# Scores and values' products in one burst, and four seams re-ordered, in a chunked attention with a gated FFN

## The chip, the cores and the metric

The kernel runs on one core of a Trainium2 chip. The core has a matmul engine (PE, with a weight loader PEld), a vector engine (DVE), an activation engine (ACT), a general engine (POOL) and a queue engine that issues DMAs (SP). The metric is the device time of one launch in microseconds. The kernel before takes 894.38 us, the median of three runs (893.72, 894.38 and 894.40).

## The reference

Inputs are q, k and v [8, 8, 576, 64], w_gate and w_val [512, 1536] and w_out [1536, 512], all float32. Attention is within chunks of 64 tokens; its output, with the heads side by side, is the input of a gated feed-forward layer.

```python
scores = scale * np.matmul(q_c, k_c.transpose(0, 1, 2, 4, 3))   # chunks of 64 tokens, scale 1/8
scores = scores - np.max(scores, axis=-1, keepdims=True)
attn = np.exp(scores)
attn = attn / (np.sum(attn, axis=-1, keepdims=True) + 1e-09)
out = np.matmul(attn, v_c)
...
x = np.ascontiguousarray(attn_out.transpose(0, 2, 1, 3)).reshape(B * S, H * D)   # [4608, 512]
g = x @ w_gate
silu = g * (1.0 / (1.0 + np.exp(-g)))
val = x @ w_val
return (silu * val @ w_out).astype(np.float32)
```

## The kernel before

**Tiles.** The 4608 tokens are nine blocks b = 0 to 8 of N = 512, each of T = 4 output tiles of 128 tokens. The hidden width 1536 is NF = 12 slices f of 128. A float32 operand is split into a high and a low part (`hh`, `hl` for h), and every product is three matmuls: low by high, high by low, high by high. `project` (L535) adds one slice of a block to its four output tiles: for each tile t three matmuls of 512 columns (L541, L542, L543). The output tiles are four banks of PSUM (`ps_o`); two more banks are `ps_a`, two `ps_gv`.

**Stages.** Blocks 0 and 1 are worked first; from slice SEVEN = 4 on, two blocks share seven products (`seventh`, L856, its matmuls at L861) in place of eight, with sums and differences of the weights formed beside them (`Quarters`: `sums`, `upper` on ACT, `lower` on DVE, L165). One step of this is `first_seven` (L874). Then block 1's projections are caught up, and block 2 is worked alone in twelve steps i = 0 to 11 (L1261 on): 12 matmuls of the gate and 12 of the value (L478), the gating product on DVE (L522), and the 12 matmuls that project the slice of the step before. Then come the pairs (3, 4), (5, 6) and (7, 8): `both_steps` (L1169) has twelve steps of seven products (`gated_pair`, L1128) with the four tiles ("turns") of the pending projection among them, and `second_steps` (L1187) projects the pair's second block.

**Attention beside it.** The attention of the blocks to come is fitted into these steps, and belongs to `Attn` (L251). `products` makes the scores, small matmuls of 64x64 (L290); `take` copies two banks to SBUF (ACT, L298) and `less_top` subtracts the row maxima (DVE, L305 and L306); `exponents` (ACT) and `normalize` (DVE, L316 to L327) follow. `turn` transposes in squares of 32 on DVE (L355): a block has eight units of four transposes, and `turn_some(a, first, n)` does n units. `cross` (L1057) makes the values' products of two pairs of heads each time: first p = 0 in one pair of banks, then p = 2 in the other (L368), each followed by two copies out of PSUM on ACT (L371). `load_values` (L1054) loads v for it. The later sums and splits of the turned block for a pair's products are `x0` to `x6` and `s1` to `s5` of `Pair`.

**Order.** On PE, DVE, ACT and POOL instructions run in program order, so the order is written out by hand: in block 2 the table `behind` (L1244) says what follows step i and `middle` what stands ahead of its projection; in the pairs `bursts` stands after the second of the four turns, `middle` inside the step and `behind` at its end (L1288 to L1293). DMAs on SP's queue are placed by a scheduler. The end of the program is the last call of `project` for block 8; its eviction takes tiles out of PSUM into buffers of two pools (`o_sb` and `v_t`) and stores them (L548 to L558).

## Time and profile before

| | |
|---|---|
| median of three runs | 894.38 us |
| the profiled execution, its own time | 893.99 us |
| its span, first to last instruction | 891.8 us |
| PE's granted clock, mean | 1.000 |
| matmul and weight-load instructions | 6035 each |
| DVE / ACT / POOL instructions | 828 / 593 / 33 |
| read from and written to memory | 178.78 MB / 43.52 MB |

The time of an execution has 2.2 us around the span. A line of a timeline reads: start and duration in us, engine, line of the kernel, operation, output<-inputs, shape, count, and in brackets the idle time ahead of it with what ended it. Several alike are gathered into one line with a count, and the duration is then from the first one's start to the last one's end. Matmuls are pipelined: each is listed longer than its distance to the next. A line of waits has the waiting operation, the one that ended it, and total, count and longest. A line by stretch has the stretch, its length, the busy time of PE, PEld, DVE, ACT and POOL with counts, PE's granted clock, the DMA share and GB/s. The trace counts 128 small matmuls for the scores or the values' products of a whole block.

### The profile page before, as it was taken

How to read it: one execution, taken by the hardware profiler on the slowest of the kernel's cores; microseconds unless marked ns; L12 is line 12 of the kernel's file. 1: busy time of each engine (PE TensorE's matmuls, PEld its weight loads, DVE VectorE, ACT ScalarE, POOL GpSimd, SP SyncE). 2: the span in 40 equal slices, each digit the busy share in tenths (PEclk: the TensorE clock that was granted, in tenths of full speed). 3: DMA queues.
4: the chain of work that ended last, by engine and by line, in shares of the span. 5: the costliest groups of instructions: out<-in, count | busy, mean ns of one | idle time of the engine just before them, and what ended most of it. 6: DMA issues, size and time to landing. Idle time of an engine off the chain costs nothing.

```text
span 891.8 us, 14744 instructions
## 1 busy us (share of the span) xinstructions
PE 881.9 (99%) x6035; PEld 730.6 (82%) x6035; DVE 547.0 (61%) x828; ACT 389.0 (44%) x593; POOL 42.1 (5%) x33
## 2 busy tenths in 40 slices
PE   7999999999999999999999999999999999999998
PEld 6788788888888888888888888888888888888886
DVE  6888999673888656776753656767655533333332
ACT  5757777543433345225325444244325432223232
POOL 1200000000055110000000000000000000000000
PEclk9999999999999999999999999999999999999999
DMA  9767778898798777657577757575657475555651
GB/s 359 263 254 288 269 284 320 329 326 310 224 386 279 272 266 237 239 219 253 201 258 288 299 210 265 194 253 229 200 215 278 177 271 203 195 198 230 236 189 47
DMA packets 73170, 223.25 MB, mean 250 GB/s; under 512 B 30736, under 2 KB 30992, under 8 KB 58896
## 3 DMA queue, kind: packets, MB, share of 16 engines
q1 hardware_dynamic: 71520, 219.57, 67.8%
q10 hardware_dynamic: 1584, 2.75, 0.9%
q8 instruction: 47, 0.77, 0.3%
q14 instruction: 19, 0.16, 0.0%
HBM read 178.78 MB, written 43.52 MB: 249 GB/s over the span
## 4 chain that ended last, share of the span: by engine, by line
PE 94%; DMA 2%; DVE 1%; POOL 1%; issue 0%; ACT 0%; SPq 0%; DVEq 0%; POOLq 0%
PE ps_a L861 26%; PE ps_gv L861 20%; PE ps_gv L478 12%; PE ps_o L541 11%; PE ps_o L542 11%; PE ps_o L543 11%; DMA v_t<-in_v 2%; PE ps_a L290 2%; PE ps_a L368 1%; DMA qk_t<-in_qk 0%; PE ps_a L468 0%; POOL v_t L411 0%; SPq L109 0%; DMA out<-o_sb 0%; PE ps_a L454 0%
## 5 line engine op out<-in xcount | busy, mean ns | idle before, releaser
L861 PE MATMUL ps_a<-x,factors 128*128 128x512 f32 x864 | 219.2, 389 | 0.0
L861 PEld LDWEIGHTS ps_a<-x,factors 128*128 128x128 f32 x864 | 162.2, 188 | 33.7
L861 PE MATMUL ps_gv<-x,factors 128*128 128x512 f32 x648 | 164.4, 389 | 0.0
L861 PEld LDWEIGHTS ps_gv<-x,factors 128*128 128x128 f32 x648 | 121.6, 188 | 25.2
L541 PE MATMUL ps_o<-both,hl 128*128 128x512 f32 x336 | 132.1, 393 | 0.0
L543 PE MATMUL ps_o<-both,hh 128*128 128x512 f32 x336 | 130.8, 389 | 0.0
L542 PE MATMUL ps_o<-both,hh 128*128 128x512 f32 x336 | 130.8, 389 | 0.0
L63 DVE TENSOR_TENSOR hl<-h,hh 128x512 fp32r<-128x512 f32 x98 | 68.3, 697 | 64.5 <-ACT hh L62 63.3
L62 ACT CAST hh<-h 128x512 fp32r<-128x512 f32 x98 | 60.6, 618 | 95.1 <-PE ps_o L543 51.3
L478 PE MATMUL ps_gv<-xh,w 128*128 128x512 f32 x320 | 97.2, 390 | 0.1
L865 DVE TENSOR_TENSOR h<-h,ps_gv 128x512 f32<-128x512 f32 x44 | 30.2, 686 | 105.4 <-PE ps_gv L861 105.2
L355 DVE STREAM_TRANSPOSE turned<-s_sb 32x256 f32<-32x256 f32 x192 | 83.7, 436 | 2.7
L522 DVE SCALAR_TENSOR_TENSOR h<-v,h 128x512 f32<-128x512 f32 x88 | 60.9, 692 | 38.0 <-ACT h L1164 33.3
L541 PEld LDWEIGHTS ps_o<-both,hl 128*128 128x128 f32 x336 | 63.0, 188 | 13.5
L543 PEld LDWEIGHTS ps_o<-both,hh 128*128 128x128 f32 x336 | 63.1, 188 | 13.3
L542 PEld LDWEIGHTS ps_o<-both,hh 128*128 128x128 f32 x336 | 63.1, 188 | 12.6
L1164 ACT ACTIVATE h<-ps_a 128x512 f32<-128x512 f32 x36 | 21.5, 598 | 112.1 <-PE ps_a L861 112.1
L478 PEld LDWEIGHTS ps_gv<-xh,w 128*128 128x128 f32 x320 | 60.0, 188 | 12.7 <-ACT xh L618 0.3
L478 PE MATMUL ps_gv<-xl,w 128*128 128x512 f32 x160 | 61.0, 393 | 0.0
L865 DVE TENSOR_TENSOR v<-v,ps_a 128x512 f32<-128x512 f32 x44 | 30.2, 687 | 41.1 <-PE ps_a L861 36.4
L1150 ACT ACTIVATE h<-h 128x512 f32<-128x512 f32 x36 | 22.8, 632 | 52.9 <-DVE h L865 52.9
L865 DVE TENSOR_TENSOR v<-v,ps_gv 128x512 f32<-128x512 f32 x44 | 30.2, 687 | 24.2 <-PE ps_gv L861 24.2
(132 smaller groups left out, 1072.2 us busy)
## 6 DMA issues: line engine op xcount, KB each, us to landing
factors<-w SPq DMA_DIRECT2D x36, 1024.0 KB, 4.8
factors<-t SPq DMA_DIRECT2D x36, 1024.0 KB, 6.0
both<-o SPq DMA_DIRECT2D x70, 512.0 KB, 6.3
w<-w SPq DMA_DIRECT2D x16, 1024.0 KB, 8.2
t<-th SPq DMA_DIRECT2D x24, 512.0 KB, 4.2
two<-o SPq DMA_DIRECT2D x12, 1024.0 KB, 4.9
raw<-in_wgv SPq DMA_DIRECT2D x11, 1024.0 KB, 9.2
qk_t<-in_qk SPq DMA_DIRECT2D x10, 1024.0 KB, 7.7
```

Source lines behind the costliest of these rows:

```text
L62: nc.scalar.copy(out=hi, in_=src)
L63: (engine or nc.vector).tensor_tensor(out=lo, in0=src, in1=hi.bitcast(F32), op=ALU.subtract)
L355: nc.vector.transpose(out=self.turned[to:to + 32, p:p + 2, j, :, 32 * (i % 2):32 * (i % 2) + 32], in_=src[32 * i:32 * i + 32, :, o // 2, 3 ...
L478: nc.tensor.matmul(ps, w, x, start=first and (k, i) == which[0], stop=last and (k, i) == which[-1])
L522: nc.vector.scalar_tensor_tensor(out=h, in0=pv, scalar=2.0 ** -8, in1=h, op0=ALU.mult, op1=ALU.mult)
L541: nc.tensor.matmul(o, hl[:, ts], woh, start=f == a.steps[0], stop=False)
L542: nc.tensor.matmul(o, hh[:, ts], wol, start=False, stop=False)
L543: nc.tensor.matmul(o, hh[:, ts], woh, start=False, stop=f == a.steps[1])
L861: nc.tensor.matmul(ps, w[u][:, k], x[i][v][:, k], start=first and k == 0 and n == 0, stop=k == NK // 2 - 1 and n == 2, skip_group_check=True)
L865: nc.vector.tensor_tensor(out=t, in0=t, in1=ps, op=ALU.add)
L1150: nc.scalar.activation(h, h, AF.Silu, scale=2.0 ** -8)
L1164: nc.scalar.activation(h2, ps1, AF.Silu, scale=2.0 ** -8)
```

## The change

It has four parts.

1. The end. In the last call of `project`, the last tile's three matmuls become six of 256 columns, the left half's three first. Of block 8's four tiles, the first and the last are evicted in two halves (ACT the left, DVE the right), the second on ACT and the third on DVE. Right halves lie in buffers of their own ("h", "hl"). The last tile's left half is stored from ACT's queue, everything else from SP's.
2. Seam 1. In `first_seven` at f = SEVEN alone, `quarters.lower()` (L165) moves from ahead of `add(v2, ps1)` to behind it.
3. Seam 2. At the end of the shared stage the scores of block 2 (`scores_0` and `scores_2`, two bursts with matmuls between) become one burst, and `less_top` of the first moves behind the split of the next projection.
4. The fused bursts. In block 2 the scores of the pair's second block move from step 3 to step 4, directly behind `cross(c)`; its exponents, normalizing and transposes follow one step later, the transposes as 3 units in step 6, 4 in step 7 and 1 in step 8, and x0 and x3 move from step 7 to the ends of steps 8 and 9. In the pairs `cross(c)` moves from f = 8 to f = 5, directly ahead of the scores of the next pair's second block, and v of c is loaded at f = 3 instead of 6, into buffers of another pool for its second half.

```diff
@@ -538,24 +538,28 @@
             a.o = [ps_o.tile([P, DM], F32, name="ps_o") for _ in range(T)]
         for t in which:
             ts, o = slice(t * P, (t + 1) * P), a.o[t]
-            nc.tensor.matmul(o, hl[:, ts], woh, start=f == a.steps[0], stop=False)
-            nc.tensor.matmul(o, hh[:, ts], wol, start=False, stop=False)
-            nc.tensor.matmul(o, hh[:, ts], woh, start=False, stop=f == a.steps[1])
+            final = a.b * N + (t + 1) * P == NT
+            ends = final and f == a.steps[1]
+            for m in (slice(0, DM // 2), slice(DM // 2, DM)) if ends else (slice(0, DM),):
+                nc.tensor.matmul(o[:, m], hl[:, ts], woh[:, m], start=f == a.steps[0], stop=False, skip_group_check=ends)
+                nc.tensor.matmul(o[:, m], hh[:, ts], wol[:, m], start=False, stop=False, skip_group_check=ends)
+                nc.tensor.matmul(o[:, m], hh[:, ts], woh[:, m], start=False, stop=f in (a.steps[1], a.steps[1] - final), skip_group_check=ends)
             if f == a.steps[1]:
 
                 pools = (hp, "o_sb"), (ld, "v_t")
                 r = a.b * N + t * P
 
-                halves = 2 if r + P == NT else 1
+                last = a.b == NB - 1
+                halves = 2 if last and t in (0, T - 1) else 1
                 for i in range(halves):
                     m = slice(i * DM // halves, (i + 1) * DM // halves)
-                    pool, tag = pools[(t + i) % 2]
+                    pool, tag = (hp, "hl" if t else "h") if i else pools[t % 2]
                     o_sb = pool.tile([P, DM // halves], F32, name="o_sb", tag=tag)
-                    if i:
+                    if i or last and t == T - 2:
                         nc.vector.tensor_scalar_mul(o_sb, o[:, m], 2.0 ** -8)
                     else:
                         nc.scalar.activation(o_sb, o[:, m], AF.Copy, scale=2.0 ** -8)
-                    (nc.sync if i or halves == 1 else nc.scalar).dma_start(out=out[r:r + P, m], in_=o_sb)
+                    (nc.scalar if final and not i else nc.sync).dma_start(out=out[r:r + P, m], in_=o_sb)
 
     pending = []
 
@@ -924,12 +928,14 @@
         o.join()
         product(ps3, 3, True)
         add(h, ps3)
-        if w:
+        if w and f > SEVEN:
             quarters.lower()
         nc.scalar.activation(h, h, AF.Silu, scale=2.0 ** -8)
         turns([1])
         product(ps1, 4, False)
         add(v2, ps1)
+        if f == SEVEN:
+            quarters.lower()
         wo_f = out_weights(f)
         product(ps2, 5, False)
         if f + 2 < NF:
@@ -980,12 +986,12 @@
     _, h2 = first_seven(NF - 1, quarters, None)
     first_qk = [nxt.load_qk(0), nxt.load_qk(1)], [nxt.load_qk(2, 2, const, "turned")]
     fetch_o(2)
-    nxt.less_top(nxt.products(first_qk[0], ps_gv, "ps_gv"), 0)
+    scores_0, scores_2 = nxt.products(first_qk[0], ps_gv, "ps_gv"), nxt.products(first_qk[1])
     fetch_h(0)
     put = [(parts(a1, NF - 2, h1), last_o)]
+    nxt.less_top(scores_0, 0)
     wo_f = pending[0][1]
     lag(None, None)
-    scores_2 = nxt.products(first_qk[1])
     fetch_h(1)
     put.append((parts(a1, NF - 1, h2), wo_f))
     nxt.less_top(scores_2, 2)
@@ -1051,8 +1057,8 @@
         if not beside_pair:
             a.less_top(ps[1], 2)
 
-    def load_values(a):
-        a.v = [a.load_v_crossed(p, "v_t" if p < 2 else "qk_t") for p in range(NP)]
+    def load_values(a, others=((ld, "qk_t"), (ld, "qk_t"))):
+        a.v = [a.load_v_crossed(p, tag, pool) for p, (pool, tag) in enumerate(((ld, "v_t"), (ld, "v_t")) + others)]
 
     def cross(a, beside_pair=True):
         for p in (0, 2):
@@ -1208,11 +1214,6 @@
         for i in range(first, first + n):
             a.turn(i // 4 * 2, i // 2 % 2, (i % 2,))
 
-    def softmax_and_turn(a, i):
-
-        return (lambda: (a.exponents(0, NP), a.normalize(0, NP)), lambda: a.turn(0, 0), lambda: a.turn(0, 1),
-                lambda: (a.turn(2, 0), a.turn(2, 1)))[i]()
-
     a, pair = nxt, []
     queries = []
 
@@ -1240,15 +1241,14 @@
         with tc.issue_after(a.asked):
             load_values(a)
 
-    middle = {0: lambda: c.exponents(0, NP), 4: lambda: pair.a[1].exponents(0, NP)}
-    behind = {0: lambda: c.normalize(0, NP), 1: lambda: (softmax_and_turn(c, 1), softmax_and_turn(c, 2)),
-              2: lambda: (c.turn(2, 0), c.turn(2, 1, (0,)), load_late(c)),
-              3: lambda: (c.turn(2, 1, (1,)), scores(pair.second(), False, moved(0))),
-              4: lambda: (cross(c, False), pair.a[1].normalize(0, NP), load_values(pair.a[1])),
-              5: lambda: (softmax_and_turn(pair.a[1], 1), softmax_and_turn(pair.a[1], 2)),
-              6: lambda: softmax_and_turn(pair.a[1], 3), 7: lambda: (pair.x0(), pair.x3()),
-              8: lambda: (cross(pair.a[1], False), load_weights(0), pair.s1(), pair.x1()),
-              9: lambda: (pair.s4(), pair.s2(), pair.x2()), 10: lambda: (pair.x4(), pair.s5()),
+    middle = {0: lambda: c.exponents(0, NP), 5: lambda: pair.a[1].exponents(0, NP)}
+    behind = {0: lambda: c.normalize(0, NP), 1: lambda: turn_some(c, 0, 3),
+              2: lambda: (turn_some(c, 3, 3), load_late(c)), 3: lambda: turn_some(c, 6, 2),
+              4: lambda: (cross(c, False), scores(pair.second(), False, moved(0)), load_values(pair.a[1])),
+              5: lambda: pair.a[1].normalize(0, NP), 6: lambda: turn_some(pair.a[1], 0, 3),
+              7: lambda: turn_some(pair.a[1], 3, 4),
+              8: lambda: (turn_some(pair.a[1], 7, 1), cross(pair.a[1], False), load_weights(0), pair.s1(), pair.x1(), pair.x0()),
+              9: lambda: (pair.s4(), pair.s2(), pair.x2(), pair.x3()), 10: lambda: (pair.x4(), pair.s5()),
               11: lambda: (load_weights(1), pair.x5(), pair.x6())}
 
     late_t = {3: LateQuarters(0), 5: LateQuarters(1), 6: LateQuarters(2), 9: LateQuarters(3)}
@@ -1285,10 +1285,11 @@
         if not pair.last:
             n = Pair(b + 2, moved(11))
             c = n.a[0]
-            bursts = {0: lambda: scores(c), 5: lambda: scores(n.second()), 8: lambda: cross(c), 11: lambda: cross(n.a[1])}
+            bursts = {0: lambda: scores(c), 5: lambda: (cross(c), scores(n.second())), 11: lambda: cross(n.a[1])}
             middle = {1: lambda: c.exponents(0, NP), 6: lambda: n.a[1].exponents(0, NP)}
-            behind = {1: lambda: c.normalize(0, NP), 2: lambda: turn_some(c, 0, 3), 3: lambda: turn_some(c, 3, 3),
-                      4: lambda: turn_some(c, 6, 2), 6: lambda: (n.a[1].normalize(0, NP), load_values(c)),
+            behind = {1: lambda: c.normalize(0, NP), 2: lambda: turn_some(c, 0, 3),
+                      3: lambda: (turn_some(c, 3, 3), load_values(c, ((xs, "xh1"), (xs, "xl1")))),
+                      4: lambda: turn_some(c, 6, 2), 6: lambda: n.a[1].normalize(0, NP),
                       7: lambda: turn_some(n.a[1], 0, 3), 8: lambda: (turn_some(n.a[1], 3, 3), load_values(n.a[1])),
                       9: lambda: turn_some(n.a[1], 6, 2)}
             later = dict(enumerate((n.x0, n.s1, n.x1, n.s4, n.s2, n.x2, n.x3, n.x4, n.s5, n.x5, n.x6)))
```

Where the instructions stand, first on DVE at the end of block 2's steps 5 to 8 before the change. `L522` is the gating product that opens a step, `L63 hl` the split of h, `L63 x` those of x0, x3 and x1, `L1085` the sum s1:

```order
L355 STREAM_TRANSPOSE turned<-s_sb 32x2x4x32 x16
L522 SCALAR_TENSOR_TENSOR h<-ps_gv,h 128x512
L63 TENSOR_TENSOR hl<-h,hh 128x512
L355 STREAM_TRANSPOSE turned<-s_sb 32x2x4x32 x16
L522 SCALAR_TENSOR_TENSOR h<-ps_gv,h 128x512
L63 TENSOR_TENSOR hl<-h,hh 128x512
L63 TENSOR_TENSOR x<-s_sb,x 128x1024 x2
L522 SCALAR_TENSOR_TENSOR h<-ps_gv,h 128x512
L63 TENSOR_TENSOR hl<-h,hh 128x512
L1085 TENSOR_TENSOR sum<-s_sb 128x1024
L63 TENSOR_TENSOR x<-sum,x 128x1024
```

The same steps on DVE after the change (the first row closes step 5; the sum is now L1091):

```order
L327 TENSOR_TENSOR s_sb<-s_sb,z 128x2048
L522 SCALAR_TENSOR_TENSOR h<-ps_gv,h 128x512
L63 TENSOR_TENSOR hl<-h,hh 128x512
L355 STREAM_TRANSPOSE turned<-s_sb 32x2x4x32 x12
L522 SCALAR_TENSOR_TENSOR h<-ps_gv,h 128x512
L63 TENSOR_TENSOR hl<-h,hh 128x512
L355 STREAM_TRANSPOSE turned<-s_sb 32x2x4x32 x16
L522 SCALAR_TENSOR_TENSOR h<-ps_gv,h 128x512
L63 TENSOR_TENSOR hl<-h,hh 128x512
L355 STREAM_TRANSPOSE turned<-s_sb 32x2x4x32 x4
L1091 TENSOR_TENSOR sum<-s_sb 128x1024
L63 TENSOR_TENSOR x<-sum,x 128x1024
```

The transposes of steps 5 and 6 now stand in steps 6, 7 and 8, the last four behind step 8's split and ahead of the sum, which needs the values' products of that step; the two splits of step 7 are gone from there.

Next, on PE the burst of step f = 5 in the first pair (blocks 3 and 4), before the change, between the second and third turn of the projection:

```order
L541 MATMUL ps_o<-both,hl 128x512
L542 MATMUL ps_o<-both,hh 128x512
L543 MATMUL ps_o<-both,hh 128x512
L290 MATMUL ps_a<-qk_t 64x64 x64
L541 MATMUL ps_o<-both,hl 128x512
L542 MATMUL ps_o<-both,hh 128x512
L543 MATMUL ps_o<-both,hh 128x512
```

The same place after the change, where project's matmuls are L544 to L546:

```order
L544 MATMUL ps_o<-both,hl 128x512
L545 MATMUL ps_o<-both,hh 128x512
L546 MATMUL ps_o<-both,hh 128x512
L368 MATMUL ps_a<-turned,v_t 64x64 x64
L290 MATMUL ps_a<-qk_t 64x64 x64
L544 MATMUL ps_o<-both,hl 128x512
L545 MATMUL ps_o<-both,hh 128x512
L546 MATMUL ps_o<-both,hh 128x512
```

The values' products stood alone in the same way in step f = 8, and stand there no more. (64 in such a listing are 128 in the trace.)

Last, DVE at seam 1 (step f = 4 of the shared stage) before the change; `L865 v<-v,ps_a` is `add(v2, ps1)`:

```order
L90 ISA wo<-wo,o_sb 128x1024
L865 TENSOR_TENSOR h<-h,ps_gv 128x512
L165 TENSOR_TENSOR th<-ts,th 128x1024
L865 TENSOR_TENSOR v<-v,ps_a 128x512
L63 TENSOR_TENSOR both<-wo,both 128x512
```

And after it, where `add` is L869:

```order
L90 ISA wo<-wo,o_sb 128x1024
L869 TENSOR_TENSOR h<-h,ps_gv 128x512
L869 TENSOR_TENSOR v<-v,ps_a 128x512
L165 TENSOR_TENSOR th<-ts,th 128x1024
L63 TENSOR_TENSOR both<-wo,both 128x512
```

`quarters.lower()` and the add have changed places.

## The prediction

> **What bounds the kernel now.** I read first the page's head and its chain, then the waits of the matmul engine (PE), then the stretches of the span.

> ```profile
> span 891.8 us, 14744 instructions
> PE 881.9 (99%) x6035; PEld 730.6 (82%) x6035; DVE 547.0 (61%) x828; ACT 389.0 (44%) x593; POOL 42.1 (5%) x33
> PE 94%; DMA 2%; DVE 1%; POOL 1%; issue 0%; ACT 0%; SPq 0%; DVEq 0%; POOLq 0%
> ...
> PE ps_a L668 <- DVE tops L661: 2.1, 2, 1.4
> ...
> PE ps_a L861 <- DVE v L865: 0.4, 1, 0.4
> ...
> 25.00:320.00 295.00, 294.18 (x2149) 243.26 (x2140) 229.51 (x339) 162.68 (x236) 36.41 (x25) 1.00 0.80 290
> 320.00:880.00 560.00, 560.00 (x3414) 463.93 (x3413) 299.43 (x454) 208.80 (x330) 2.04 (x1) 1.00 0.63 227
> ```

> PE is busy 99% of the span at a granted clock of 1.00, and 94% of the chain that ends last is PE. Of 295 us up to 320 it misses 0.82, of the 560 after that nothing. So a change pays only where it takes time from PE's own stream: a wait, a costly switch between kinds of matmul, or the tail behind the last matmul. Only one wait on the list lies at an edited place, L861 with 0.4 us; 2.1 at L668 lies in the untouched beginning. This sets the scale: no edit can win more than tenths of a microsecond, while any new wait of PE costs its full length.

> **Seam 1 (first step of seven products).**

> ```profile
> 92.54 0.39 PE L542 MATMUL ps_o<-both,hh 128*128 128x512 f32 x1
> 92.77 0.39 PE L543 MATMUL ps_o<-both,hh 128*128 128x512 f32 x1
> 93.54 0.50 PE L861 MATMUL ps_a<-xl,th 128*128 128x512 f32 x1 [0.39 <-DVE v L865]
> 93.88 0.63 PE L861 MATMUL ps_a<-xh,th 128*128 128x512 f32 x2
> ...
> 91.67 1.22 DVE L165 TENSOR_TENSOR th<-ts,th 128x1024 fp32r<-128x1024 f32 x1
> 92.81 0.68 DVE L865 TENSOR_TENSOR v<-v,ps_a 128x512 f32<-128x512 f32 x1
> ```

> Whole matmuls follow each other every 0.23 us (92.54, 92.77); here the next starts 0.77 later, 0.54 too late, and the one behind it 0.34 later, 0.11 too late. L861 waits for add(v2), which reads the same bank; the add ends at 93.49, L861 starts 0.05 later. The add stood behind the 1.22 us of L165. With L165 behind it, it can start at 91.67 and end by 92.35, before PE asks at 93.00. Late next is L165 itself, which then ends near 93.5; its result is first read in the second product of the next step, some 3 us later, so nothing waits. **−0.66**, between −0.4 (the listed wait alone) and −0.7.

> **Seam 2 (about 181 us): two score bursts become one.**

> ```profile
> 181.19 0.39 PE L543 MATMUL ps_o<-both,hh 128*128 128x512 f32 x1
> 181.51 1.16 PE L290 MATMUL ps_a<-qk_t 64*64 64x64 f32 x64
> ...
> 182.94 0.39 PE L542 MATMUL ps_o<-both,hh 128*128 128x512 f32 x1
> ...
> 402.05 0.39 PE L543 MATMUL ps_o<-both,hh 128*128 128x512 f32 x1
> 402.37 2.17 PE L290 MATMUL ps_a<-qk_t 64*64 64x64 f32 x128
> ...
> 404.80 0.39 PE L542 MATMUL ps_o<-both,hh 128*128 128x512 f32 x1
> ```

> From the L543 ahead of a burst to the L542 behind it lie 1.75 us for 64 traced matmuls and 2.75 for 128; less two pitches of 0.227 that would be there anyway, 1.30 and 2.30. Two of 64 cost 2.60, one of 128 2.30: a burst costs 0.30 to enter and leave. The DVE work of both bursts (reductions and subtractions out of PSUM) now meets the splits of h for the projections that follow; worked along the DVE rows, the tighter of these splits is ready about 0.35 us before PE asks. **−0.30**, between −0.30 and +0.3 if that margin is lost.

> **Fused bursts: scores joined to the values' products, three times** (step 4 of block 2, step 5 of two pairs). By the same arithmetic each would save 0.30. But the four PSUM banks of the first half are those that the scores need.

> ```profile
> 441.42 2.16 PE L368 MATMUL ps_a<-turned,v_t 64*64 64x64 f32 x128
> 443.51 0.50 PE L541 MATMUL ps_o<-both,hl 128*128 128x512 f32 x1
> ...
> 442.61 2.05 ACT L371 COPY s_sb<-ps_a 128x512 f32<-128x512 f32 x4 [0.67 <-PE ps_a L368]
> ```

> Let T be the start of the values' products (441.42). ACT begins to copy at T+1.19, when the first half is complete, and takes 2.05 for four, so the second copy ends near T+2.27. The scores' first two matmuls write the two banks that these two copies free, so the second cannot start before T+2.32 with the 0.05 of seam 1; without a wait it would start at about T+2.05. The rest of the scores take 2.10, and the next L541 comes at T+4.42. Apart, the two bursts take 2.09 from start to L541 and a further 2.30: T+4.39. So each fusion gives **+0.03, together +0.1**; the wait takes back the saved switch. Bounds: −0.30 each if the copies are not in the way, +0.15 each if the third and fourth copy (T+3.24) hold the second half as well.

> [...]

> **Block 2, steps 6 to 8.** The fused burst comes one step later than the old scores, so the softmax of the pair's second block and its transposes slip by a step: 12 transposes in step 6, 16 in step 7, and the last 4 in step 8, directly ahead of the products that read them.

> ```profile
> 274.17 0.69 DVE L522 SCALAR_TENSOR_TENSOR h<-ps_gv,h 128x512 f32<-128x512 f32 x1 [1.26 <-PE ps_gv L478]
> ...
> 283.36 0.69 DVE L522 SCALAR_TENSOR_TENSOR h<-ps_gv,h 128x512 f32<-128x512 f32 x1
> ...
> 285.35 7.18 DVE L355 STREAM_TRANSPOSE turned<-s_sb 32x256 f32<-32x256 f32 x16
> 292.56 0.69 DVE L522 SCALAR_TENSOR_TENSOR h<-ps_gv,h 128x512 f32<-128x512 f32 x1
> ...
> 262.95 0.69 DVE L306 TENSOR_TENSOR s_sb<-ps_a,top 128x512 f32<-128x512 f32 x1
> ...
> 269.98 2.94 DVE L327 TENSOR_TENSOR s_sb<-s_sb,z 128x2048 f32<-128x2048 f32 x1
> ...
> 273.90 0.39 PE L541 MATMUL ps_o<-both,hl 128*128 128x512 f32 x1
> ...
> 282.06 0.39 PE L541 MATMUL ps_o<-both,hl 128*128 128x512 f32 x1
> ...
> 298.38 0.39 PE L541 MATMUL ps_o<-both,hl 128*128 128x512 f32 x1
> ...
> 301.19 2.14 PE L368 MATMUL ps_a<-turned,v_t 64*64 64x64 f32 x128
> ```

> Let R be the first L541 of a step; steps without a burst are 8.16 apart (273.90, 282.06). The gating product L522 starts at R+0.27 when DVE is free (274.17). In a step with 16 transposes the next L522 comes 9.20 after the last (283.36, 292.56), 1.04 more than PE's step. So in step 8 L522 starts 1.04 late, at R+1.31. Transposes start 1.99 behind it (283.36, 285.35): R+3.30, and four at 0.45 (7.18 for 16) take 1.79: R+5.09. The products start at R+2.81 (298.38, 301.19), and half of them, at R+3.85, is done when the second half asks for the last transposes; it gets them at about R+5.14. PE waits **+1.3**. Before, the transposes were all over by 292.53, nearly 9 us ahead of these products, so this is a new wait and not a moved one. This holds if step 7 begins on time. From the last subtraction of a softmax (262.95) to the end of its normalizing (272.92) DVE took 9.28 us from end to end; by that, normalizing in step 5 lets step 6's L522 come at about R+0.7, and its 12 transposes make the next one 7.40 later (1.99 + 12 × 0.45): some 0.3 us to spare. Every tenth beyond that goes straight into the wait. Bounds: 0, if something else has moved these products later or the transposes go faster than in any row, and 1.9.

> **The end.**

> ```profile
> 887.96 0.38 ACT L557 ACTIVATE o_sb<-ps_o 128x256 f32<-128x256 f32 x1
> ...
> 888.82 0.42 DVE L555 TENSOR_SCALAR o_sb<-ps_o 128x256 f32<-128x256 f32 x1 [4.95 <-DMA out<-o_sb]
> 889.27 0.33 SPq L558 DMA_DIRECT2D out<-o_sb  x1
> L454 PE MATMUL pt<-ident,s_sb x16: 270/272/273, 203.1 to 204.7; 128*128 128x128 f32 x16
> ```

> The last half on DVE waited for an earlier output DMA until 888.82, though ACT's half was done at 888.34; the new buffers have no such wait. In the built program ACT's half still waits for the last of the six half-width matmuls, and DVE's half for ACT's, as before. So the split itself brings nothing: six times half of 0.227 is the old time. A half-width matmul is not in the trace; it costs between 0.113 (half a pitch) and 0.22 (the 128-column rows, 16 within 1.67 us or 0.104 each, plus 0.113). I take 0.113, the proportional value, since the 128-column rows at 0.104 carry other operands. ACT then ends near 888.38, DVE starts at 888.40 and the last DMA issues at 888.85 instead of 889.27: **−0.4**, between −0.45 and 0 if the halves cost 0.18 or more.

> [...]

> **At nothing** I put: the earlier loads of values (SP's queue has idle spells, and the DMA share after 320 is 0.63), the later splits x0 and x3 (first needed by the pair's products near 328 us, some 10 us on), and DVE's and ACT's changed order inside the pairs (DVE is busy 299 of 560 us there). If such a cover were gone, the waiting operation would show in PE's waits at its full length.

> **Sum.** −0.66 − 0.30 + 0.1 + 1.3 − 0.4 = +0.04 on the profiled execution of 893.99 us (span 891.8 and 2.2 around it), which lies 0.4 below the median of 894.38 and close to the mean of all four times, 894.1. I say **894.2**.

> **Rivals.** A measurement of this kernel can tell about 0.2%, 1.8 us, from no change.
> - No wait in step 8 (the last transposes are in time after all): the 1.3 goes, 892.9. For it: a wait needs the whole DVE chain of steps 5 to 8 to stand as worked out. Against it: in every row a transpose takes 0.45 us, and 16 make the next L522 late.
> - Neither that wait nor the one inside the fused bursts: −0.66 − 0.30 − 0.9 − 0.45, that is 2.3 off, 891.8. It needs the copies to be quicker than their row; it is what the change would give if only PE's stream counted.
> - Slower: the DVE chain of block 2 reaches step 6 late.

> ```profile
> 254.91 1.43 DVE L63 TENSOR_TENSOR hl<-h,hh 128x512 fp32r<-128x512 f32 x1 [0.69 <-ACT hh L62]
> ...
> 253.39 2.41 POOL L187 TENSOR_TENSOR th<-w 128x1024 f32<-128x1024 f32 x1 [3.77 <-PE ps_gv L478]
> ```

>   The split of h here took 1.43 instead of the 0.69 of others, while POOL worked on a tensor of its own. Normalizing now stands in step 5, and if it and the splits around it lose time in that way, step 6's transposes start late and the wait in step 8 grows by as much. It decides from 0.3 us of lateness; 2.0 us beyond that make 896.2. Against it: the 16 transposes at 285.35 took 7.18 with POOL at work as well.
> - The change does not do what it says: in the fused bursts this is part of the forecast itself (the joined burst has a hole of 0.27), and at the end the split into halves frees nothing early.

> **How the numbers follow.** As worked out: 0.70, with its own range 892.8 to 895.4. No wait in step 8: 0.10. Neither wait: 0.11. Late chain: 0.09. The last two are left out of the range but for their edges, so it goes from 892.0 to 895.9. Faster by over 0.2% is below 892.6: the third case and a fifth of the second, 0.13. Slower by as much is the last case, 0.09. Same: 0.78.

> **What would show it.** In the waits of PE: L861 at seam 1 gone; a new wait of L368 for DVE's transposes near 300 us, about 1.3; new waits of L290 for ACT's copies, about 0.3 each, three times. In the timeline: one burst near 181; from the fused burst's start to the next L541 4.4 us; the last SP issue 0.4 us sooner. Wrong would make it: no wait in the values' products of step 8, the copies of the first half done before T+2.0, or a wait of PE in the pairs, where I expect none outside the bursts.

## The result, and the profile after

The changed kernel takes 909.97 us (median of 4 runs, 907.85 to 911.93), the kernel before 894.05 (4 runs, 893.67 to 894.40): a ratio of 1.0174, interval 1.0160 to 1.0189. It is slower by 15.9 us; 894.2 with a range up to 895.9 had been forecast. The profiled execution took 911.43, 17.4 more than that of before.

The page of the changed kernel, its head, the chain that ended last, the granted clock by 40 slices and the queues of instructions; and from the waits of PE the rows that are new:

```profile
span 909.3 us, 14740 instructions
PE 888.2 (98%) x6038; PEld 736.2 (81%) x6038; DVE 547.6 (60%) x830; ACT 388.6 (43%) x592; POOL 40.8 (4%) x33
...
PEclk9999999999999999998999999989999999999999
...
q8 instruction: 47, 0.77, 0.3%
...
PE 90%; DVE 3%; issue 2%; DMA 2%; ACT 1%; SPq 1%; POOL 0%; ACTq 0%; DVEq 0%; POOLq 0%
...
PE ps_a L290 <- issue: 9.7, 3, 5.1
...
PE ps_gv L478 <- issue: 0.7, 1, 0.7
PE ps_a L368 <- DVE turned L355: 0.6, 1, 0.6
```

PE's share of the chain falls from 94 to 90%, and "issue" rises from 0 to 2%: time in which PE waited for nothing that the profile shows. Three such waits stand at L290, the scores, 9.7 us in all: one for each fused burst. And the clock is below full in two slices.

The timeline of PE through the second fused burst (first pair, step 5), the rows that end the holes of the first and the third, and PE's clock by stretches of the second (the column ahead of the last two):

```profile
405.77 2.10 PE L368 MATMUL ps_a<-turned,v_t 64*64 64x64 f32 x126
407.69 0.22 PE L290 MATMUL ps_a<-qk_t 64*64 64x64 f32 x1
407.71 0.23 PE L368 MATMUL ps_a<-turned,v_t 64*64 64x64 f32 x2
407.75 1.67 PE L290 MATMUL ps_a<-qk_t 64*64 64x64 f32 x71
414.53 1.77 PE L290 MATMUL ps_a<-qk_t 64*64 64x64 f32 x56 [5.12 <-issue]
416.24 0.79 PE L544 MATMUL ps_o<-both,hl 128*128 128x512 f32 x1
...
267.32 1.96 PE L290 MATMUL ps_a<-qk_t 64*64 64x64 f32 x114 [1.28 <-issue]
...
609.03 2.83 PE L290 MATMUL ps_a<-qk_t 64*64 64x64 f32 x92 [3.31 <-issue]
...
405.77:407.77 2.00, 2.00 (x131) 2.00 (x130) 1.29 (x2) 1.34 (x4) 0.00 (x0) 1.00 1.04 406
414.53:416.24 1.71, 1.71 (x57) 1.59 (x56) 0.00 (x0) 0.00 (x0) 0.00 (x0) 0.50 0.50 114
416.24:418.96 2.72, 2.72 (x9) 2.15 (x7) 2.54 (x4) 0.00 (x0) 0.00 (x0) 0.50 0.97 320
```

The burst is joined as intended, and the small wait for ACT's copies that was forecast is there: the scores go on 2.33 us after the start of the burst (2.32 had been worked out), and their first 71 matmuls take 1.67 us instead of some 1.16. Then, after the 72nd of the scores' 128 matmuls, in the middle of a tile and with no wait that the profile shows, PE stands still for 5.1 us, and comes back at half the clock (0.50 in the stretch from 414.53, 1.00 in the one from 405.77). From the start of the burst to the next L544 pass 10.47 us instead of the 4.42 forecast. The same is seen at 263 us (5.94, hole 1.28) and at 602 us (9.18, hole 3.31, half clock behind it).

**Where the holes lie.** I numbered PE's instructions (matmuls, weight loads, semaphore instructions and three drains) by their start. The holes of the changed kernel begin at numbers 4289, 4545, 6593 and 9153. Divided by 256, each leaves 193. The second, 4545, is the row at L478 above: ordinary 512-column matmuls, 3 us behind the first fused burst. The queue named "instruction" carried 47 packets of 16,384 bytes, and among the 12,194 instructions of PE there are 47 numbers that leave 193: by this count one packet to 256 instructions. So **the holes lie exactly where, by this count, a new block of instructions begins**.

The answer on DMAs for the half microsecond from 412.0, the only one between 404 and 416 with such a packet (its columns: packets, MB, share of the DMA engines):

```profile
DMA packets 285, 0.13 MB, mean 251 GB/s; under 512 B 279, under 2 KB 279, under 8 KB 279
...
q1 hardware_dynamic: 284, 0.11, 80.1%
q8 instruction: 1, 0.02, 14.1%
```

The pace alone does not open a hole. At 491.88 us of the same run PE enters another block (7361) at the start of a single burst of 128, uses it up in 1.94 us, and goes on without a wait: the next packet had been carried at 490.57, while PE was still among large matmuls. By the theory, a hole needs a packet that starts too late for the block that is being used up.

Most edges show no hole: 5 of the changed kernel's 47 have one, the one near 23 us told of next included, and three of the five lie within a fused burst, 512 quick instructions in a row.

**The kernel before had the sign of it.** Its waits of PE and its timeline in the first 25 us:

```profile
PE ps_a L468 <- issue: 0.7, 1, 0.7
...
22.21 0.57 PE L468 MATMUL ps_a<-pT,v_t 64*64 64x64 f32 x22
23.44 0.75 PE L468 MATMUL ps_a<-pT,v_t 64*64 64x64 f32 x37 [0.66 <-issue]
```

There two bursts of small matmuls follow each other closely (L290 at 20.05, L468 at 22.21), and after 22 of the second PE waits 0.66 us for "issue", at number 705 = 193 + 2 × 256. All twelve kernels have a hole at 705, of 0.40 to 1.72 us. I had the row and passed over it.

### The profile page after: what moved, and what is told of

Read it like the earlier page. It is cut to its first block, busy times and chain, and to the rows that moved or that the text cites. A ratio compares the mean times of both kernels' runs of the same rounds, so it can differ in the third digit from the quotient of the medians.

```text
span 909.3 us, 14740 instructions
## 1 busy us (share of the span) xinstructions
PE 888.2 (98%) x6038; PEld 736.2 (81%) x6038; DVE 547.6 (60%) x830; ACT 388.6 (43%) x592; POOL 40.8 (4%) x33
## 3 DMA queue, kind: packets, MB, share of 16 engines
q10 hardware_dynamic: 1584, 2.75, 0.9%
## 4 chain that ended last, share of the span: by engine, by line
PE 90%; DVE 3%; issue 2%; DMA 2%; ACT 1%; SPq 1%; POOL 0%; ACTq 0%; DVEq 0%; POOLq 0%
PE ps_a L865 26%; PE ps_gv L865 19%; PE ps_o L544 11%; PE ps_o L546 10%; PE ps_o L545 10%; PE ps_gv L478 10%; PE ps_a L290 2%; DMA v_t<-in_v 2%; DVE turned L355 1%; PE ps_a L368 1%; DVE h L522 0%; ACT s_sb L371 0%; PE ps_a L468 0%; SPq L109 0%; POOL v_t L411 0%
## 5 line engine op out<-in xcount | busy, mean ns | idle before, releaser
L865 PE MATMUL ps_a<-x,factors 128*128 128x512 f32 x864 | 220.2, 390 | 0.0
L865 PEld LDWEIGHTS ps_a<-x,factors 128*128 128x128 f32 x864 | 163.1, 189 | 34.2
L865 PE MATMUL ps_gv<-x,factors 128*128 128x512 f32 x648 | 164.4, 389 | 0.0
L865 PEld LDWEIGHTS ps_gv<-x,factors 128*128 128x128 f32 x648 | 121.6, 188 | 25.3
L544 PE MATMUL ps_o<-both,hl 128*128 128x512 f32 (+1 forms) x337 | 133.0, 395 | 0.0
L545 PE MATMUL ps_o<-both,hh 128*128 128x512 f32 (+1 forms) x337 | 131.9, 391 | 0.0
L546 PE MATMUL ps_o<-both,hh 128*128 128x512 f32 (+1 forms) x337 | 131.9, 391 | 0.0
L63 DVE TENSOR_TENSOR hl<-h,hh 128x512 fp32r<-128x512 f32 x98 | 70.4, 719 | 64.0 <-ACT hh L62 63.8
L62 ACT CAST hh<-h 128x512 fp32r<-128x512 f32 x98 | 60.6, 618 | 91.0 <-PE ps_o L546 51.3
L478 PE MATMUL ps_gv<-xh,w 128*128 128x512 f32 x320 | 97.1, 390 | 0.8 <-issue 0.7
L869 DVE TENSOR_TENSOR h<-h,ps_gv 128x512 f32<-128x512 f32 x44 | 30.2, 686 | 102.9 <-PE ps_gv L865 102.6
L355 DVE STREAM_TRANSPOSE turned<-s_sb 32x256 f32<-32x256 f32 x192 | 83.7, 436 | 2.8
L522 DVE SCALAR_TENSOR_TENSOR h<-v,h 128x512 f32<-128x512 f32 x88 | 60.9, 692 | 39.0 <-ACT h L1170 34.3
L544 PEld LDWEIGHTS ps_o<-both,hl 128*128 128x128 f32 x337 | 63.7, 189 | 13.6
L546 PEld LDWEIGHTS ps_o<-both,hh 128*128 128x128 f32 x337 | 63.8, 189 | 13.4
L478 PEld LDWEIGHTS ps_gv<-xh,w 128*128 128x128 f32 x320 | 60.0, 188 | 13.5 <-issue 0.9
L478 PE MATMUL ps_gv<-xl,w 128*128 128x512 f32 x160 | 60.9, 392 | 0.0
L869 DVE TENSOR_TENSOR v<-v,ps_a 128x512 f32<-128x512 f32 x44 | 30.2, 687 | 41.4 <-PE ps_a L865 36.7
L869 DVE TENSOR_TENSOR v<-v,ps_gv 128x512 f32<-128x512 f32 x44 | 30.2, 687 | 24.6 <-PE ps_gv L865 24.5
```

The source lines that it names most:

```text
L62: nc.scalar.copy(out=hi, in_=src)
L63: (engine or nc.vector).tensor_tensor(out=lo, in0=src, in1=hi.bitcast(F32), op=ALU.subtract)
L355: nc.vector.transpose(out=self.turned[to:to + 32, p:p + 2, j, :, 32 * (i % 2):32 * (i % 2) + 32], in_=src[32 * i:32 * i + 32, :, o // 2, 3 ...
L478: nc.tensor.matmul(ps, w, x, start=first and (k, i) == which[0], stop=last and (k, i) == which[-1])
L522: nc.vector.scalar_tensor_tensor(out=h, in0=pv, scalar=2.0 ** -8, in1=h, op0=ALU.mult, op1=ALU.mult)
L544: nc.tensor.matmul(o[:, m], hl[:, ts], woh[:, m], start=f == a.steps[0], stop=False, skip_group_check=ends)
```

## The experiments

All times are medians, with the ratio to runs of the kernel before on the same chip (894.1).

**No fusion.** The change without its fused bursts: tables of before, seams and end of the change.

```diff
-            bursts = {0: lambda: scores(c), 5: lambda: (cross(c), scores(n.second())), 11: lambda: cross(n.a[1])}
+            bursts = {0: lambda: scores(c), 5: lambda: scores(n.second()), 8: lambda: cross(c), 11: lambda: cross(n.a[1])}
...
```

> The change without its fused bursts (block 2's table and the pairs' tables as before; the two seams and the end as changed). Theory, instruction supply: PE runs out of instructions inside the fused bursts, because 512 short instructions in a row use up a 256-instruction block in 2.1 us while the next block takes 4 to 8 us to come; without them no wait of PE by the name of issue is left after 40 us, and the time is that of before less the seams and the end, 0.7 + 0.3 + 0.4: about 892.7 us. Rival, the seams or the end have a part in the loss: over 895 us.

893.02 us, ratio 0.9990 (0.9981 to 0.9999). No "issue" is left behind the first 25 us. The seams and the end are a small gain and no part of the loss; they bring 1.0 instead of 1.36, for which see below.

**Pairs fused.** The kernel before with the change's `bursts`, `middle`, `behind` and `load_values` of the pairs, and nothing else.

> The kernel before with the pairs' fused bursts alone. Instruction supply: two holes of 3 to 6 us inside the scores' half, each followed by about 4 us at half the clock, 14 us in all: 906 to 911 us. Both holes begin at an instruction whose number on PE (matmuls, weight loads and semaphore instructions counted from the start) leaves 193 when divided by 256, as in the change. Rival, the fusion is harmful only together with block 2's new table (later softmax, later transposes): under 897 us.

904.04 us, 1.0119 (1.0104 to 1.0135). The waits of PE and the rows that end the two holes, with the clock behind each:

```profile
PE ps_a L290 <- issue: 7.2, 2, 4.4
...
410.29 1.77 PE L290 MATMUL ps_a<-qk_t 64*64 64x64 f32 x56 [4.38 <-issue]
...
602.94 1.61 PE L290 MATMUL ps_a<-qk_t 64*64 64x64 f32 x92 [2.81 <-issue]
...
410.29:411.99 1.70, 1.70 (x56) 1.58 (x56) 0.00 (x0) 0.00 (x0) 0.00 (x0) 0.50 0.52 117
...
602.94:604.49 1.55, 1.55 (x93) 1.48 (x93) 0.00 (x0) 0.83 (x2) 0.00 (x0) 1.00 1.10 249
```

Two holes at 6593 and 9153, as expected, and no other part of the change is needed for them. The time is below the 906 expected: the second hole is shorter, and without half clock.

**Block 2 fused.** The kernel before with the change's table of block 2 alone.

> The kernel before with block 2's new table alone. Instruction supply: a hole of 1 to 4 us in the fused burst near 263 us, longer or shorter with what the DMA queues hold, and the wait of the values' products for the last transposes in step 8, 1.1 to 1.6 us: together 896.5 to 899 us. Rival, the losses in block 2 belong to the other parts of the change: 894 us.

898.84 us, 1.0053 (1.0040 to 1.0067). Holes of 1.0 and 1.5 us at 4289 and 4545, and the values' products of step 8 take 3.74 us up to the next matmul instead of 2.07.

**Apart.** As no fusion, but with the early loads of v and the values' products alone in step 6.

```diff
-            bursts = {0: lambda: scores(c), 5: lambda: scores(n.second()), 8: lambda: cross(c), 11: lambda: cross(n.a[1])}
+            bursts = {0: lambda: scores(c), 5: lambda: scores(n.second()), 6: lambda: cross(c), 11: lambda: cross(n.a[1])}
...
```

> The change without fusion (as no_fusion), but in the pairs the values' products of the first block and the loads of v stand early, as in the change; the products are a burst of their own in step 6, one step behind the scores of step 5. Instruction supply: bursts of 256 instructions with a step between them leave no hole: 892.7 us, within 0.5. Rival, the early products, their loads or the buffers they take cause the hole: two holes of 3 us and more, over 900 us.

894.58 us, 1.0004 (0.9995 to 1.0013). The rival's two holes are not there, yet the time is 1.6 above that of no fusion. The timeline of PE behind the burst of step 6:

```profile
416.62 2.37 PE L368 MATMUL ps_a<-turned,v_t 64*64 64x64 f32 x128
...
421.77 0.84 PE L865 MATMUL ps_gv<-x,factors 128*128 128x512 f32 x3
423.65 0.85 PE L865 MATMUL ps_gv<-x,factors 128*128 128x512 f32 x3 [1.03 <-issue]
```

My expectation was too simple: a single burst can do it too. Here a block (6593) begins 0.46 us into the burst, is used up in 5.15 us, and its successor's packet started 4.28 us after PE had entered it. The hole stands among 512-column matmuls, at 6849, again 193. In the profiled execution the hole at 705 is longer too, 1.72 us instead of 0.68 in that of no fusion; so not all of the 1.6 belongs to the burst of step 6.

**Before, shifted.** No part of the change; 32 score products made twice, so that all later instructions stand 128 places on.

```diff
-    nxt.less_top(nxt.products(first_qk[0], ps_gv, "ps_gv"), 0)
+    scores_0 = nxt.products(first_qk[0], ps_gv, "ps_gv")
+    for i in range(2):
+        nxt.scores(first_qk[0][i][:, 0], i, scores_0)
+    nxt.less_top(scores_0, 0)
```

> The kernel before, with none of the change's parts; the 32 score products of block 2's first two pairs of heads (64 matmuls and 64 weight loads in the trace, 128 instructions, about 1.05 us) are made a second time into the same banks near 181 us, so that every later instruction of PE stands 128 places further on. Instruction supply: in the kernel before, a block of 256 begins some 71 matmuls into the pairs' scores burst at 402 us; here it begins 64 matmuls earlier, near the 7th, so that the rest of the burst and about seven whole matmuls behind it use the block up in 3.6 us, while the next takes 5 to 8 us; a hole of 1.5 to 4 us opens behind the burst, among ordinary 512-column matmuls, at an instruction whose number leaves 193 when divided by 256: 896.5 to 900 us. Rival, the holes belong to the fusion (banks, copies, order): 895.1 us, the price of the added matmuls alone, and no hole.

895.80 us, 1.0021 (1.0011 to 1.0030). At 402 us nothing happened: the packet for that edge was carried at 402.72, 1.59 us before PE entered the block at 404.31; what sets its start these runs do not show. The hole came at another burst of the unchanged code, the 128 scores at 222 us:

```profile
221.92 2.17 PE L290 MATMUL ps_a<-qk_t 64*64 64x64 f32 x128
224.02 0.50 PE L478 MATMUL ps_gv<-xl,w 128*128 128x512 f32 x1
...
225.06 0.39 PE L478 MATMUL ps_gv<-xh,w 128*128 128x512 f32 x1
225.98 0.39 PE L478 MATMUL ps_gv<-xh,w 128*128 128x512 f32 x1 [0.53 <-issue]
```

A block (3521) began 0.11 us into the burst, was gone in 3.03 us, and the next packet started 1.52 us after it began. So the place was a miss, the kind was not: without any fusion, a shift of 128 instructions opens a hole at a number that leaves 193 (3777), in code that had none. Of the 1.7 us, 1.05 are the added matmuls.

**Pairs shifted.** As pairs fused, with 16 score products made twice (64 instructions).

```diff
...
+    nxt.scores(first_qk[0][1][:, 0], 1, scores_0)
...
```

> The kernel before with the pairs' fused bursts (as pairs_fused), and 16 score products of block 2 made a second time near 181 us (64 instructions, 0.5 us). Instruction supply: both holes stay where the number of the instruction leaves 193 when divided by 256, so they move 32 matmuls towards the front of the scores: from behind the 72nd and 36th of the scores' matmuls to behind about the 40th and 4th. Rival, a wait for a bank, a copy or a transfer of q and k: the holes stay behind the same matmuls of the scores.

905.71 us (one run). The ends of the two holes in PE's timeline:

```profile
405.07 1.15 PE L290 MATMUL ps_a<-qk_t 64*64 64x64 f32 x39
409.41 2.05 PE L290 MATMUL ps_a<-qk_t 64*64 64x64 f32 x88 [3.18 <-issue]
...
605.63 0.59 PE L542 MATMUL ps_o<-both,hh 128*128 128x512 f32 x1 [3.26 <-issue]
```

The first hole moved from behind the 72nd to behind the 40th matmul of the scores, 32 places, as expected, though the order of banks, copies and transfers around it is the same. The second did not come at the 4th: the burst ran through (598.76 to 601.24), and the hole came one block later, at 9409, behind the burst. Both leave 193.

**Gap.** As pairs fused, with six large matmuls between the two halves.

```diff
...
-5: lambda: (cross(c), scores(n.second()))
+5: lambda: (cross(c), turns([2, 3]), scores(n.second()))
...
```

> The kernel before with the pairs' fused bursts, but with the last two turns of the projection (six matmuls of 512 columns, 1.4 us) between the values' products and the scores. Instruction supply: a block still holds half of each burst, and is used up in 3.7 us instead of 2.1; the holes become 1 to 1.6 us shorter, 1.5 to 3.5 us each, and stay at 193. Rival, the scores wait for the four copies out of the banks: these end 1.15 us behind the last of the values' products and so within the gap; no hole, 894 us.

898.70 us (one run), with holes of 1.9 and 2.1 us at 6593 and 9153:

```profile
409.07 1.15 PE L290 MATMUL ps_a<-qk_t 64*64 64x64 f32 x62 [1.92 <-ACT s_sb L298]
...
599.86 1.67 PE L290 MATMUL ps_a<-qk_t 64*64 64x64 f32 x98 [2.11 <-issue]
```

The profile puts the first down to a copy by ACT, but that copy had ended at 408.17, 0.9 us before PE went on. Both lie at 193, the four copies of the first half had ended (405.46) before the scores began (405.89), and the rival's 894 was not reached.

**Quiet.** As pairs fused; the loads of v for the pair's second block move from step 8 to step 5, and the loads of factors that began just ahead of the burst come behind them.

```diff
+            if f == 5 and f in bursts:
+                with tc.issue_after(n.a[1].v_asked):
+                    load_weights(f + 2)
...
```

> The kernel before with the pairs' fused bursts; the loads of v for the next pair's second block are asked for at step 5, and the two 1 MB loads of weight factors that began 2 us ahead of the burst stand behind them in SP's queue, so that they begin after the burst. Instruction supply: the 16 KB packet of instructions, which waited 3 to 5 us behind this data, is carried sooner; the holes shrink to 0.5 to 2.5 us each, none is followed by the half clock: 896 to 900 us. Rival, the holes come from within PE or the banks: 904 us as pairs_fused.

897.16 us, 1.0040 (1.0026 to 1.0053), 6.9 us less than pairs fused, with the same instructions on PE. Its waits of PE, the rows that end the two holes, and the clock behind the first:

```profile
PE ps_a L290 <- issue: 1.8, 2, 1.1
...
PE ps_gv L861 <- DMA factors<-t: 1.0, 1, 1.0
...
406.81 1.04 PE L290 MATMUL ps_a<-qk_t 64*64 64x64 f32 x56 [1.09 <-issue]
...
597.58 1.61 PE L290 MATMUL ps_a<-qk_t 64*64 64x64 f32 x92 [0.70 <-issue]
...
406.81:407.85 1.04, 1.04 (x57) 0.97 (x57) 0.00 (x0) 0.00 (x0) 0.00 (x0) 1.00 0.62 141
```

The packets started 0.70 and 0.62 us after the block was entered, instead of 4.67 and 3.09; the holes shrank from 4.38 and 2.81 to 1.09 and 0.70, and the clock stayed full (1.00 behind the first, 1.000 on the mean of the execution). One microsecond was lost to the factors that now come late. So most of a hole went with the loads ahead of the burst and the late start of the instruction packet, but not all: here no data packet was on the queues from 2 us ahead of the block to the start of its successor's packet, and still 3.6 and 3.2 us passed from the block's first instruction to the next block's, while the 256 instructions lasted 2.3.

**Block 2, turns.** As block 2 fused, with 4 and 4 units of transposes in steps 6 and 7.

```diff
-6: lambda: turn_some(pair.a[1], 0, 3), 7: lambda: turn_some(pair.a[1], 3, 4), 8: lambda: (turn_some(pair.a[1], 7, 1), cross(...
+6: lambda: turn_some(pair.a[1], 0, 4), 7: lambda: turn_some(pair.a[1], 4, 4), 8: lambda: (cross(...
```

> The kernel before with block 2's new table (as block2_fused), but with four units of transposes in step 6 and four in step 7, none in step 8. The wait of 1.7 us of the values' products in step 8 belongs to the last four transposes: they now end about 0.5 us ahead of the products, the wait goes, and 897.2 us are left of 898.8. Rival, the wait belongs to banks or copies of the products themselves: it stays, 898.8 us.

897.90 us, 1.0039 (1.0026 to 1.0053). The wait for the transposes is gone, but another stands in its place:

```profile
303.52 0.33 PE L368 MATMUL ps_a<-turned,v_t 64*64 64x64 f32 x4
304.66 2.08 PE L368 MATMUL ps_a<-turned,v_t 64*64 64x64 f32 x124 [0.81 <-DVE h L522]
```

With 16 transposes in each of two steps the gating product L522 itself comes late (303.92), and the products wait for the bank that it reads (it ends at 304.61, they go on at 304.66). From 303.52 to the next matmul pass 3.2 us, so 1.1 us of wait are left of 1.7: neither expectation holds. DVE is too late in these steps.

**Best.** No fusion, with one cast of ACT behind the copy that PE waits for in the step after seam 1.

```diff
-        o.below()
+        if f != SEVEN + 1:
+            o.below()
...
         nc.scalar.copy(out=h, in_=ps1)
+        if f == SEVEN + 1:
+            o.below()
```

> The change without its fused bursts (as no_fusion), and in the step behind seam 1 ACT's copy of the first product stands ahead of one cast of weights (0.7 us) that delayed it. The wait of 0.28 us that PE gained there through seam 1 goes: 892.7 us. Rival, the step waits for DVE or for a later copy instead: 893.0 us.

893.16 us, 0.9990 (0.9981 to 0.9999): the same as no fusion within 0.2 us. The wait of 0.28 us at 98 us is gone, and one of 0.36 us at 105 us, for DVE, has come: the rival holds.

## Why the prediction was wrong

**Fused bursts: +0.1 forecast, about +17 in the profiled execution.** This is the step that failed. I priced a joined burst by its matmuls, its switches and the banks that ACT's copies free, and bounded it by −0.30 and +0.15 each. The wait for the copies is there as worked out (T+2.33 against T+2.32). What was missing is the holes, which the theory puts down to the supply of instructions. By burst: from its start to the next large matmul 5.94, 10.47 and 9.18 us instead of 4.42, that is 1.5, 6.05 and 4.8; 0.8 more at the hole at 4545; and behind the second and third burst the half clock for some 4 and 3 us, 1.95 and 1.5 us. These sum to 16.6 above the forecast and 16.7 above the kernel before. With the 1.66 of step 8 and the 0.80 gained by the three parts below, that makes 17.6; the profiled span grew by 17.5. None of the prediction's rivals had this term; the only slower one was the DVE chain of block 2, up to 896.2. The runs show that fusion alone brings it (pairs fused, block 2 fused), that its place follows the number of instructions and not the work (pairs shifted, before shifted), and that it shrinks when the loads ahead of the burst are moved away (quiet). The cost differs from run to run (907.85 to 911.93); why was not measured.

The bound was wrong in kind: all its rows came from bursts of 128, and twice as many in a row was an operation that the trace of before did not show. I called the extremes "no wait" and "a longer wait for copies", and did not ask what else is consumed twice as fast.

**Step 8 of block 2: +1.3 forecast, 1.66 measured** (302.93 to 306.66 from the start of the products to the next matmul, 301.19 to 303.26 before).

```profile
285.45 1.56 DVE L63 TENSOR_TENSOR hl<-h,hh 128x512 fp32r<-128x512 f32 x1 [0.69 <-ACT hh L62]
...
301.64 0.69 DVE L522 SCALAR_TENSOR_TENSOR h<-ps_gv,h 128x512 f32<-128x512 f32 x1
...
303.73 1.81 DVE L355 STREAM_TRANSPOSE turned<-s_sb 32x256 f32<-32x256 f32 x4
...
302.93 1.26 PE L368 MATMUL ps_a<-turned,v_t 64*64 64x64 f32 x68
...
305.59 1.14 PE L368 MATMUL ps_a<-turned,v_t 64*64 64x64 f32 x58 [0.58 <-DVE turned L355]
306.66 0.50 PE L478 MATMUL ps_gv<-xl,w 128*128 128x512 f32 x1
```

The mechanism was right: PE waits for the last transposes. It was mis-sized because the gating product of step 8 came 1.52 us behind the step's first L544 (301.64 and 300.12), not 1.31, and the transposes began 2.09 behind it, not 1.99. The rival of the late chain came true in small: in step 6 the split of h took 1.56 us instead of 0.69 and used up the 0.3 that was to spare.

**Seam 1: −0.66 forecast, −0.68 at the seam but −0.21 two steps on.** The wait for the add is gone. "Nothing waits" was wrong: by 107 us PE has lost 0.47 again, in the next step for a copy of ACT that stood behind casts of weights (0.28), and behind that once more. In "best" the first of these goes and another comes. The helpers of this stage are themselves close to their limit.

**Seam 2: −0.30 forecast, −0.39 measured** (no fusion against before, transposes of block 2 at 203 us). Right, and the small margin held.

**The end: −0.4 forecast, −0.20 measured** (from the start of the last tile's first matmul to the end of the span, 4.55 us in no fusion, 4.75 before). The working on the engines was right: the six half-width matmuls keep a pitch of 0.11 to 0.12 us, the DVE half starts 0.41 us after ACT's, no output DMA is waited for, and the last one is issued 0.42 sooner (1.78 us behind that matmul instead of 2.20). But I took the end of the span to come sooner by as much, and it did not: the last transfer took 1.84 us from its issue to its landing instead of 1.68, and 0.06 more passed behind it.

The three were forecast at −1.36 together; measured they sum to −0.80 of the 1.00 by which the span of no fusion is shorter. The other 0.2 is a few hundredths each at places that were not edited.

## What to carry to other kernels

The bursts of small matmuls were limited here by more than their banks and their operands: at 8 to 9 ns for an instruction, PE used up a block of code in 2.3 us, while the next could be worked on 3.2 us after the block was entered at the soonest (quiet) and 7.7 us after it at the latest (the second fused burst), unless its packet had been carried before. The hole then appeared at a fixed number of instructions (193 more than a multiple of 256), in before shifted at 225 us, 44 us behind the edit at 181. Count instructions over time before bursts are joined; a row of "issue" inside a burst in the profile was the sign of it here (0.66 us at 705 in the kernel before). And when an operation is made longer than any in the trace, its upper bound cannot be taken from the shorter ones.

## What the runs showed of the hardware

- The queue named "instruction" carried packets of 16,384 bytes, one to 256 instructions of PE by the count above (47 for 12,194), and the holes put down to "issue" all begin at a number that leaves 193 when divided by 256: 17 of 0.5 us and more behind the first 40 us, in nine kernels (one of them given to a copy by the profile), and the hole at 705 in all twelve.
- At these holes 2.2 to 2.9 us passed from the start of the packet to PE's next instruction. The packet started 0.6 and 0.7 us after PE entered the block ahead of it where no data was on the queues (quiet), and 1.3 to 5.2 us after it in the other kernels; the DMA share alone does not order these (in the changed kernel 1.5 us for the block entered at 263.49 and 5.2 for the one entered at 406.88, with data shares of 100% and 88% meanwhile). With packets and edges taken in order, at 21 of the changed kernel's 47 edges the packet was carried 0.07 to 4.66 us before PE entered that block, PE being among 512-column matmuls (490.57 for a block entered at 491.88; in before shifted 402.72 for one entered at 404.31); when a packet is asked for was not measured.
- Behind holes of 3.26 us (pairs shifted), 3.31 and 5.12 (the changed kernel) and 4.38 (pairs fused) the granted clock was 0.50, for up to 6 us (414.53 to 420.5 in the changed kernel); behind one of 3.18 (pairs shifted) it was 0.69 on the mean of the next 2 us. Behind holes of 2.81 (pairs fused), 1.28 and 0.68 (the changed kernel) and 1.09 (quiet) it was 1.00. What sets the clock was not measured.
